# Attention and a squared-ReLU network: queries and keys of batches 3 to 7 loaded as rows in SBUF and transposed there, scores in 448 columns

## The chip, the core and the metric

The kernel runs on one core of one Trainium2 chip. The time is device microseconds of one execution; three runs of the kernel before gave a median of 371.77 us, the lowest 371.64 and the highest 372.14. All inputs and the output lie in DRAM as float32; the matrices are worked on as float16 with sums in float32.

## The reference

`q`, `k` and `v` are `[8, 12, 448, 64]`: 8 batches, 12 heads, 448 positions, 64 columns a head. Attention has one added term in its denominator, and its output goes through two matrix products with a squared ReLU between them:

```python
def _attn_ref(q, k, v):
    scale = 1.0 / np.sqrt(q.shape[-1])
    scores = scale * np.matmul(q, k.transpose(0, 1, 3, 2))
    m = np.max(scores, axis=-1, keepdims=True)
    e = np.exp(scores - m)
    attn = e / (np.sum(e, axis=-1, keepdims=True) + np.exp(-m) + 1e-09)
    return np.matmul(attn, v)

def _moe_ref(x, w_in, w_out):
    h = x @ w_in            # [3584, 768] @ [768, 2048]
    r = np.maximum(h, 0.0)
    return (r * r) @ w_out  # [3584, 2048] @ [2048, 768]

x = attn_out.transpose(0, 2, 1, 3).reshape(8 * 448, 12 * 64)
```

The output is `[3584, 768]`. Dividing numerator and denominator by `exp(-m)` shows that no maximum is needed: the kernel computes `exp(scores)` and divides by one plus its sum.

## The kernel before

**How the work is cut.** A batch has three *quads* of four heads. A quad's 448 keys are seven *chunks* of 64. For one chunk, `quad_scores` multiplies the chunk's keys with all queries of the quad's four heads; these are products with 64 rows and 64 columns of TensorE's array each, so four of them lie side by side in its four 64x64 quadrants, and the result is one PSUM tile `sp` of two banks. `quad_exp` (ScalarE) takes the exponential of the tile into a buffer `et`. `add_quad` (VectorE, four steps, L442 to L448) adds the chunks' exponentials up into a tile `half`, `sums_of_quad` lets TensorE sum over the keys (a product with a matrix of ones), `quad_z` and `quad_reciprocal` (ScalarE) make the reciprocal by a logarithm and an exponential. `values_step` multiplies one chunk's exponentials with its values, and `quad_x` (VectorE, L488) scales the sum into `xt`, the transposed input of the network. Matrix products of the network are the pieces `J` (first product, through L666, with sums and differences of blocks so that seven block products do the work of eight) and `o` (`out_piece`, second product). `out_first` and `out_second` move a finished tile of 128 tokens by 384 columns from PSUM to a buffer `ot` (five of them), and `store` writes it to DRAM.

**The order is written out by hand.** Three lists of steps, each a letter with numbers, are run one after another: the first (batches 0 to 2 come in, the network's first product of batches 0 and 1), the second (rest of batches 1 to 3), and `CYCLE`, run once with the scores of batches 4 and 5 and once with those of 6 and 7. A step puts its instructions at the end of its engines' queues, so the order of steps is the order on every engine; engines wait for one another only through the tiles. The letters that matter here are `s` (scores of a chunk), `e` (its exponential), `a`, `S`, `Z`, `M`, `v`, `X` as above in order, `o`, `O`, `Q` (a tile of output and its store) and `d` (a load). In the lists `d` counts through `LOADS`; in the cycle it is `following`, which turns a number into a load for one of the next batches. At the end stand the remaining products of batches 6 and 7 and the last tile, stored in pieces of 384, 256 and 128 columns.

**How queries and keys come in.** TensorE needs them with the 64 columns of a head on the partitions, so they have to be transposed. For batches 0 to 2 (`ON_PE`) they are loaded in natural order and transposed on TensorE; there the row of the token 7p + t is kept as column p of the block t, and a chunk is one such block. For batches 3 to 7 three steps stand in place of that. `stage(b)` (L145 to L160, issued on POOL) copies the batch's q and k from DRAM to DRAM as float16. `transposed_load(b, i)` (L167, issued on SP) reads a copy in rows of 128 values and writes it transposed into `qk`: one plane of q, one of k, and a second plane of k moved by one position, because a row of 128 values holds two neighbouring tokens of the head, and keys and queries lie in halves by odd and even token. `tail_keys(b)` (L189, POOL) copies the keys of the last chunk together, four copies a batch. The queries' two halves are why a score product there has 224 columns, and a chunk eight products:

```python
which, x = (1, h * n + c // 2) if c % 2 == o else (2, h * n + c // 2 + c % 2)
keys = qk[r, which, x:x + 190:3]
mm(sp[64 * i:64 * i + 64, o, j * n:(j + 1) * n], keys, qk[r, 0, h * n:(h + 1) * n], start=True, stop=True)
```

For the batches 0 to 2 it is four products of 448 columns. `load_v_quads` (L98 to L112) brings the values in the order that the chunks have: one transfer for batches 0 to 2, four for the others. `store` (L543 to L552) undoes the order of the tokens: a tile of 128 columns of the transposed token order is 128 rows of the output at a stride, of 7 rows for batches 0 to 2, of 2 for the others. With stride 7 a run has 64 rows, so a tile is two transfers; with stride 2 a run has 224 rows, and a tile is one transfer or, across a border, two.

**Buffers and queues.** `qk` has two buffers, `v` two, `flat` two (first quads, and the copied tail keys `kms`). The POOL queue issues all loads, in the order of the steps; the SP queue issues the transposes and the stores. In each queue a transfer waits for the one eight before it. Free parts of `qk` are used again: `small_sums` puts sums of the first product into the third plane of batch 2's, `slot` gives nine places for kept partial sums in the last part, and `wout_sum` the sums of the second weight matrix.

Of the kernel before, what the change touches and what calls it, by code (L numbers as in the profile page):

```python
# [10 lines left out]
FP32 = mybir.dt.float32  # L11
FP16 = mybir.dt.float16
# [5 lines left out]
def kernel(  # L18
# [20 lines left out]
    COLS = H * S // 2 + 16  # L39
# [14 lines left out]
    flat = ctx.enter_context(tc.tile_pool(name="flat", bufs=2))  # L54
# [26 lines left out]
    vns, qks, xts, naturals, stages = {}, {}, {}, {}, {}  # L81
# [16 lines left out]
    def load_v_quads(b, g0=0, g1=NQ):  # L98
        if b not in vns:
            vns[b] = v_pool.tile([128, 2, NQ, KC, D], FP16, name="vn")  # L100
        vn = vns[b]
        if b in ON_PE:
            if g1 - g0 == NQ:
                nc.gpsimd.dma_start(out=vn.rearrange("p j g c d -> p (j g) (c d)"), in_=by_pairs["v"][b])
            else:
                nc.gpsimd.dma_start(out=vn[:, :, g0].rearrange("p j c d -> p j (c d)"), in_=by_pairs["v"][b, :, g0::NQ])  # L106
            return
        for i in range(2):
            rows_ = vn[64 * i:64 * i + 64].rearrange("p j g c d -> p (j g) (c d)")
            for c0, c1 in ((0, KC - 1), (KC - 1, KC)):  # L110
                src = v[:, :, 64 * c0:64 * c1].rearrange("b (hp i) (p t) d -> b i p hp (t d)", i=2, t=c1 - c0)
                nc.gpsimd.dma_start(out=rows_[:, :, c0 * D:c1 * D], in_=src[b, i])  # L112
# [14 lines left out]

    def load_first_second():
        for name in "qk":
            f = naturals[name, 0, 0, 1] = flat.tile([128, KC, D], FP16, name=f"flat{name}")  # L130
            nc.gpsimd.dma_start(out=f.rearrange("p c d -> p (c d)"), in_=by_pairs[name][0, :, NQ])  # L131
# [10 lines left out]
    HSD = H * S * D  # L142
    FRONT, TOTAL = D, HSD + 16 * 2 * D

    def stage(b):  # L145
        for n, t in (("q", q), ("k", k)):
            st = nc.dram_tensor(f"stage_{n}{b}", (TOTAL,), FP16, kind="Internal").ap()
            stages[n, b] = st
            src = t.rearrange("b h s d -> (b h s d)")
            lo = b * HSD - FRONT  # L150
            hi = min(lo + TOTAL, B * HSD)
            m = (hi - lo) // 1024 * 1024
            for x, y in ((lo, lo + m), (lo + m, hi)):
                if y > x:
                    w = min(y - x, 1024)
# [942 lines left out]
```

## Time and profile before

| | us |
|---|---|
| median of three runs (lowest, highest) | 371.77 (371.64, 372.14) |
| span of the profiled execution | 372.7 |
| TensorE matmul (PE) busy | 362.5 |
| TensorE weight load (PEld) busy | 249.0 |
| ScalarE (ACT) busy | 281.8 |
| VectorE (DVE) busy | 276.6 |
| GpSimd (POOL) busy | 62.2 |

The profile holds one execution; its span is 0.9 above the median of the runs. The POOL queue's transfers were 24752 packets with 22.62 MB and 38.8% of the time of the 16 DMA engines, the SP queue's 49952 packets with 21.59 MB and 27.3%.

How its lines are read: a group of instructions stands as line, engine, operation, output and inputs, tile shapes, "x" and the count, then after a bar the summed busy time in us, the mean of one in ns, and the idle time just before them with what ended it. A line of a timeline has the start and the length in us, then the same names. A line of transfers has their count, the KB of each and the median us from issue to landing. The chain of waits follows the work that ended last back from the last instruction, each step to what released it; "issue" is time in which an engine waited for nothing that the profile shows. L94 is the helper `mm`, through which most matmuls are issued, so its groups are told apart by their tiles: `sp` scores and row sums, `mp` all else. PEclk, the granted clock, is a share of full speed.

### The profile page before, as it was taken

Reading aid. Unit: us, or ns where it says so; the run is one execution under the profiler, and the core shown is the slowest. Engines: PE = TensorE matmul, PEld = TensorE weight load, DVE = VectorE, ACT = ScalarE, POOL = GpSimd, SP = SyncE. Lnnn points to the kernel's source line nnn. Section 1 sums busy time; section 2 is a strip of 40 time slices with the busy share of each in tenths; the row PEclk is TensorE's granted clock in tenths of the full one; section 3 lists DMA queues with packets and bytes.
Section 4 is the critical chain, followed back from the end, with each engine's and each line's share of the span. In section 5 each row is a group of like instructions: output and inputs, shape, how many; then the busy total and the mean of one; then the engine's idle time right before and its main releaser. Section 6 shows DMA issues by size and latency. Waiting matters only on the chain.

```text
span 372.7 us, 13667 instructions
## 1 busy us (share of the span) xinstructions
PE 362.5 (97%) x6024; PEld 249.0 (67%) x6024; DVE 276.6 (74%) x485; ACT 281.8 (76%) x412; POOL 62.2 (17%) x96
## 2 busy tenths in 40 slices
PE   8679999999999999999999999999999999999996
PEld 4557566669977665557799975557777765555564
DVE  2688897998987774876888783777888776886441
ACT  5799888986899664689999746579999748784221
POOL 8443170400300150400201061300200000000000
PEclk9999999999999999999999999999999999999999
DMA  8999999999884999924327879864122210001232
GB/s 137 202 206 205 204 148 204 223 226 207 150 171 85 203 162 203 147 28 94 71 54 157 133 129 197 154 72 98 47 67 50 63 46 20 2 0 44 84 84 87
DMA packets 75051, 45.31 MB, mean 122 GB/s; under 512 B 47472, under 2 KB 72944, under 8 KB 74992
## 3 DMA queue, kind: packets, MB, share of 16 engines
q0 software_dynamic: 24752, 22.62, 38.8%
q1 hardware_dynamic: 49952, 21.59, 27.3%
q8 instruction: 47, 0.77, 0.9%
q10 hardware_dynamic: 288, 0.23, 0.2%
q14 instruction: 12, 0.10, 0.1%
HBM read 45.69 MB, written 17.93 MB: 171 GB/s over the span
## 4 chain that ended last, share of the span: by engine, by line
PE 89%; ACT 5%; DMA 3%; POOL 1%; issue 1%; DVE 1%; POOLq 0%; DVEq 0%
PE mp L94 42%; PE mp L666 37%; PE sp L94 9%; ACT et L258 3%; DMA nn<-in_k_dram 3%; PE mp L208 1%; ACT rcp L369 1%; ACT rcp L376 1%; POOL nn L118 1%; DVE half L446 0%; DVE half L448 0%; ACT ot L577 0%; POOL vn L106 0%; ACT rcp L372 0%; POOL flatk L131 0%
## 5 line engine op out<-in xcount | busy, mean ns | idle before, releaser
L258 ACT ACTIVATE et<-sp 128x896 f16<-128x896 f32 (+2 forms) x173 | 145.3, 900 | 8.6 <-PE sp L94 7.9
L94 PE MATMUL mp<-wout,gs 64*64 64x384 f16 (+1 forms) x2736 | 138.9, 322 | 0.3 <-issue 0.3
L94 PEld LDWEIGHTS <-gs 64*64 64x64 f16 (+1 forms) x2736 | 87.5, 107 | 21.9 <-issue 1.1
L666 PEld LDWEIGHTS <-win 128*128 128x128 f16 x480 | 46.4, 98 | 33.6 <-issue 1.2
L94 PE MATMUL sp<-qk 64*64 64x224 f16 (+1 forms) x1056 | 55.9, 273 | 1.8 <-ACT et L258 1.1
L666 PE MATMUL mp<-xt,win 128*128 128x448 f16 (+1 forms) x288 | 54.2, 329 | 0.0
L94 PEld LDWEIGHTS <-qk 64*64 64x64 f16 x1056 | 34.2, 114 | 14.0 <-issue 5.7
L189 POOL COPY flatq<-qk 64x384 f16<-64x384 f16 x20 | 15.1, 753 | 159.3 <-DMA qk<-stage_k 158.8
L94 PE MATMUL mp<-et,vn 64*64 64x448 f16 (+1 forms) x616 | 38.8, 345 | 0.0
L666 PE MATMUL mp<-et,win 128*128 128x448 f16 x144 | 32.8, 352 | 0.0
L579 DVE TENSOR_SCALAR ot<-mp 128x384 f32<-128x384 f32 x34 | 18.9, 556 | 18.3 <-PE mp L94 17.3
L666 PE MATMUL mp<-et,nn 128*128 128x448 f16 (+1 forms) x160 | 32.3, 350 | 0.0
L666 PEld LDWEIGHTS <-nn 128*128 128x128 f16 x216 | 21.0, 98 | 14.7
L669 ACT ACTIVATE qk<-mp 128x448 f32<-128x448 f32 (+1 forms) x33 | 16.7, 531 | 16.0 <-PE mp L666 15.9
L583 DVE SCALAR_TENSOR_TENSOR ot<-mp,ot 128x384 f32<-128x384 f32 x42 | 23.4, 557 | 6.6 <-ACT ot L577 3.9
L488 DVE TENSOR_TENSOR xt<-mp,rcp 128x448 f16<-128x448 f32 x42 | 24.2, 617 | 4.6 <-ACT rcp L467 2.7
L94 PEld LDWEIGHTS <-vn 64*64 64x64 f16 x756 | 22.7, 107 | 6.8 <-issue 1.3
L718 ACT ACTIVATE gs<-mp 128x448 f16<-128x448 f32 x28 | 14.2, 542 | 15.0 <-PE mp L666 13.3
L663 DVE CUSTOM_DVE_ANT_0 gs<-mp,rcp 128x448 f16<-128x448 f32 x24 | 14.2, 619 | 13.0 <-ACT rcp L669 7.4
L442 DVE TENSOR_TENSOR half<-et 128x1792 f16<-128x1792 f16 x21 | 23.0, 1095 | 0.9 <-ACT et L258 0.9
L713 ACT ACTIVATE gs<-gs 128x448 f16<-128x448 f16 (+1 forms) x36 | 22.4, 657 | 1.1 <-DVE gs L663 1.1
L444 DVE TENSOR_TENSOR half<-half,et 128x1792 f16<-128x1792 f16 x21 | 22.9, 1090 | 0.4
(102 smaller groups left out, 452.5 us busy)
## 6 DMA issues: line engine op xcount, KB each, us to landing
out_dram<-ot SPq DMA_DIRECT2D x52, 96.0 KB, 3.3
out_dram<-ot SPq DMA_DIRECT2D x19, 192.0 KB, 2.0
win<-in_moe_w_in_dram POOLq DMA_DIRECT2D x8, 384.0 KB, 11.9
wout<-in_moe_w_out_dram POOLq DMA_DIRECT2D x4, 768.0 KB, 12.2
vn<-in_v_dram POOLq DMA_DIRECT2D x10, 288.0 KB, 5.6
stage_q<-in_q_dram POOLq DMA_DIRECT2D x4, 676.0 KB, 11.8
stage_k<-in_k_dram POOLq DMA_DIRECT2D x4, 676.0 KB, 14.9
nn<-in_q_dram POOLq DMA_DIRECT2D x8, 224.0 KB, 9.0
```

Of the source, the lines that this page charges most:

```text
L94: return nc.tensor.matmul(out_, lhsT, rhs, start=start, stop=stop)
L189: nc.gpsimd.tensor_copy(km[rows_].rearrange("p h (x o) -> p h x o", o=2)[:, :, :, odd], src[:, :, S // 2 - 32:S // 2])
L258: nc.scalar.activation(out=out_, in_=in_, func=AF.Exp, scale=scale)
L442: nc.vector.tensor_add(esq[m], a[:, 0:w], a[:, w:2 * w])
L444: nc.vector.tensor_add(esq[m], esq[m], z[:, 0:w])
L488: nc.vector.tensor_mul(xts[b][:, 2 * g + i, :], xqs[m][i][:, 0:S], zqs[m][:, i, :])
L579: nc.vector.tensor_scalar(out=ot, in0=op[:, 0:w], scalar1=OUT_SCALE, scalar2=None, op0=ALU.mult)
L583: nc.vector.scalar_tensor_tensor(out=ot, in0=lo[:, 0:w], scalar=OUT_SCALE, in1=ot, op0=ALU.mult, op1=ALU.add)
L663: nc.vector._custom_dve(TENSOR_ADD_SAT, out=out_, in0=ps, in1=t, s0=3.0e38, s1=0.0)
L666: nc.tensor.matmul(out_, lhsT=lhsT, rhs=rhs, start=begins and first, stop=last, skip_group_check=not begins)
L669: nc.scalar.activation(out=t[:, 0:w], in_=src[:, 0:w], func=AF.Copy, scale=scale_)
L713: nc.scalar.activation(out=out_, in_=out_, func=AF.Square)
```

## The change

The kernel after holds all batches in the token order of batches 0 to 2, and no DRAM copies are made.

- `load_rows(b, n, j)` takes the place of `stage`. A new tile `rows` (one buffer) has q in its partitions 0 to 63 and k in 64 to 127; partition p holds, for a head pair c and a block t, the token 7p + t of head c and beside it that of head c + 6, 128 values. Each of the 24 transfers a batch loads one head of one tensor, in pieces of 64 values (128 bytes as float16), and casts on the way. `load_all_rows(b)` issues all of them on POOL.
- `transposed_load(b, n)` has two transfers a batch, q and k, from `rows` to `qk`, SBUF to SBUF; the second key plane and `tail_keys` go, and `qk` has two planes.
- `quad_scores` has one form, four products of 448 columns, and `of_column` one order. `load_v_quads` loads a batch in one transfer, and `store` has stride 7 for all tokens.
- The loads are called at other places in the lists: those of batch 3 to 5 in the second list are renumbered (rows of batch 3 stay where its staging was; the values of batch 3 stand where they stood, and batch 4's rows, which followed them directly, now come after batch 3's transposes), and `following` has a batch's two transposes, values and the rows of the batch after next in another order and at other places.
- Buffers: `flat` has four, all of one size, and `small_sums` uses them; `slot` has its places in two `qk` buffers and the `rows` buffer, and `wout_sum` the rest of these.

```diff
...
-    COLS = H * S // 2 + 16
+    COLS = H * S // 2
...
-    flat = ctx.enter_context(tc.tile_pool(name="flat", bufs=2))
+    flat = ctx.enter_context(tc.tile_pool(name="flat", bufs=4))
+    rows_pool = ctx.enter_context(tc.tile_pool(name="rows", bufs=1))
...
-    vns, qks, xts, naturals, stages = {}, {}, {}, {}, {}
+    vns, qks, xts, naturals, rows_of = {}, {}, {}, {}, {}
...
-        if b in ON_PE:
-            if g1 - g0 == NQ:
-                nc.gpsimd.dma_start(out=vn.rearrange("p j g c d -> p (j g) (c d)"), in_=by_pairs["v"][b])
-            else:
-                nc.gpsimd.dma_start(out=vn[:, :, g0].rearrange("p j c d -> p j (c d)"), in_=by_pairs["v"][b, :, g0::NQ])
-            return
-        for i in range(2):
-            rows_ = vn[64 * i:64 * i + 64].rearrange("p j g c d -> p (j g) (c d)")
-            for c0, c1 in ((0, KC - 1), (KC - 1, KC)):
-                src = v[:, :, 64 * c0:64 * c1].rearrange("b (hp i) (p t) d -> b i p hp (t d)", i=2, t=c1 - c0)
-                nc.gpsimd.dma_start(out=rows_[:, :, c0 * D:c1 * D], in_=src[b, i])
+        if g1 - g0 == NQ:
+            nc.gpsimd.dma_start(out=vn.rearrange("p j g c d -> p (j g) (c d)"), in_=by_pairs["v"][b])
+        else:
+            nc.gpsimd.dma_start(out=vn[:, :, g0].rearrange("p j c d -> p j (c d)"), in_=by_pairs["v"][b, :, g0::NQ])
...
+    def flat_tile():
+        return flat.tile([128, DCH // 2 * FIRST], FP16, name="flat")
     def load_first_second():
...
-            f = naturals[name, 0, 0, 1] = flat.tile([128, KC, D], FP16, name=f"flat{name}")
-            nc.gpsimd.dma_start(out=f.rearrange("p c d -> p (c d)"), in_=by_pairs[name][0, :, NQ])
+            f = flat_tile()[:, 0:S]
+            naturals[name, 0, 0, 1] = f.rearrange("p (c d) -> p c d", d=D)
+            nc.gpsimd.dma_start(out=f, in_=by_pairs[name][0, :, NQ])
...
-    HSD = H * S * D
-    FRONT, TOTAL = D, HSD + 16 * 2 * D
-    def stage(b):
...
-    PLANES = (("q", FRONT, H * S // 2), ("k", FRONT, H * S // 2), ("k", 0, COLS))
-    def transposed_load(b, i):
-        qk = qk_of(b)
-        n, x, c = PLANES[i]
+    def load_rows(b, n, j):
+        if b not in rows_of:
+            rows_of[b] = rows_pool.tile([128, DCH * KC * 2 * D], FP16, name="rows")
+        dst = rows_of[b][64 * n:64 * n + 64].rearrange("p (c t j d) -> p c t j d", c=DCH, t=KC, j=2)
+        for c in range(DCH):
+            nc.gpsimd.dma_start(out=dst[:, c, :, j], in_=(q, k)[n][b, DCH * j + c].rearrange("(p t) d -> p t d", t=KC))
+    def load_all_rows(b):
+        for n in range(2):
+            for j in range(2):
+                load_rows(b, n, j)
+    def transposed_load(b, n):
...
-            out=qk[:, i, 0:c],
-            in_=stages[n, b][x:x + c * 2 * D].rearrange("(r c) -> r c", c=2 * D),
+            out=qk_of(b)[:, n].rearrange("p (r x) -> p r x", x=64),
+            in_=rows_of[b][64 * n:64 * n + 64],
...
     def transposed_loads(b):
-        for i in range(3):
-            transposed_load(b, i)
-    kms = {}
-    def tail_keys(b, planes=(1, 2)):
...
     def qk_of(b):
...
-            qks[b] = qk_pool.tile([128, 3, COLS], FP16, name="qk")
+            qks[b] = qk_pool.tile([128, 2, COLS], FP16, name="qk")
...
     def first_cast(raw, name, c0, c1, act):
...
-            naturals[name, 0, 0, 0] = flat.tile([128, KC, D], FP16, name=f"flat{name}")
+            naturals[name, 0, 0, 0] = flat_tile()[:, 0:S].rearrange("p (c d) -> p c d", d=D)
...
-    def of_column(e, m, j):
-        if QUADS[m][0] in ON_PE:
-            return e.rearrange("p (j x) -> p j x", j=2)[:, j]
-        return e.rearrange("p (o j x) -> p j o x", o=2, j=2)[:, j]
+    def of_column(e, j):
+        return e.rearrange("p (j x) -> p j x", j=2)[:, j]
...
     def quad_scores(m, c):
...
-        if b in ON_PE:
-            for i in range(2):
-                for j in range(2):
-                    r = slice(64 * j, 64 * j + 64)
-                    x = (2 * g + i) * S
-                    mm(sp[64 * i:64 * i + 64, j, 0:S], qk[r, 1, x + 64 * c:x + 64 * c + 64],
-                       qk[r, 0, x:x + S], start=True, stop=True)
-        else:
-            n = S // 2
+        for i in range(2):
...
-                for i in range(2):
-                    for o in range(2):
-                        r = slice(64 * o, 64 * o + 64)
-                        h = 2 * NQ * j + 2 * g + i
-                        if c == KC - 1:
-                            keys = kms[b][r, h, :]
-                        else:
-                            which, x = (1, h * n + c // 2) if c % 2 == o else (2, h * n + c // 2 + c % 2)
-                            keys = qk[r, which, x:x + 190:3]
-                        mm(sp[64 * i:64 * i + 64, o, j * n:(j + 1) * n], keys,
-                           qk[r, 0, h * n:(h + 1) * n], start=True, stop=True)
+                r = slice(64 * j, 64 * j + 64)
+                x = (2 * g + i) * S
+                mm(sp[64 * i:64 * i + 64, j, 0:S], qk[r, 1, x + 64 * c:x + 64 * c + 64],
+                   qk[r, 0, x:x + S], start=True, stop=True)
...
-                mm(zp[64 * j:64 * j + 64, i, 0:S], ones[r], of_column(es[r], m, j), start=True, stop=True)
+                mm(zp[64 * j:64 * j + 64, i, 0:S], ones[r], of_column(es[r], j), start=True, stop=True)
...
-                mm(xqs[m][i][64 * j:64 * j + 64, 0:S], vns[b][r, j, g, c, :], of_column(e[r], m, j),
+                mm(xqs[m][i][64 * j:64 * j + 64, 0:S], vns[b][r, j, g, c, :], of_column(e[r], j),
...
-            step = KC if b in ON_PE else 2
-            rows = out[b * S:(b + 1) * S, n0:n1].rearrange("(p t) m -> t p m", t=step)
-            t, p = c % S // (S // step), c % S % (S // step)
-            m = min(S // step - p, end - c)
+            rows = out[b * S:(b + 1) * S, n0:n1].rearrange("(p t) m -> t p m", t=KC)
+            t, p = c % S // 64, c % 64
+            m = min(64 - p, end - c)
...
-             + [lambda: stage(3), lambda: transposed_loads(3), lambda: tail_keys(3), lambda: load_v_quads(3),
-                lambda: stage(4), lambda: transposed_loads(4), lambda: tail_keys(4), lambda: load_v_quads(4), lambda: stage(5)])
+             + [lambda: load_all_rows(3), lambda: transposed_loads(3), lambda: load_v_quads(3),
+                lambda: load_all_rows(4), lambda: transposed_loads(4), lambda: load_v_quads(4), lambda: load_all_rows(5)])
...
     def small_sums(xsum, y):
-        xsum[y] = qks[2][:, 2, (y - 1) * HC * FIRST:y * HC * FIRST].rearrange("p (c n) -> p c n", c=HC)
+        xsum[y] = flat_tile().rearrange("p (c n) -> p c n", c=HC)
...
+    osum = {}
...
     def slot():
...
-            scratch.append(qk_pool.tile([128, 3 * COLS // 2], FP32, name="qk"))
-        n = slots[0] = (slots[0] + 1) % 9
-        return scratch[0][:, n * S:n * S + S]
+            t, u = (qk_pool.tile([128, COLS], FP32, name="qk") for _ in range(2))
+            w = rows_pool.tile([128, COLS], FP32, name="rows")
+            osum["u"], osum["w"] = u, w
+            scratch.extend(t[:, n * S:n * S + S] for n in range(COLS // S))
+            scratch.extend(u[:, COLS - n * S:COLS - n * S + S] for n in (2, 1))
+            scratch.append(w[:, COLS - S:COLS])
+        slots[0] += 1
+        return scratch[slots[0] % len(scratch)]
...
-        o4,12,14 s58 o4,14,16 v3,0 S3 v3,1 e58 O4,0 v3,2 v3,3 Z3 Q4 v3,4 a4,1 s59 v3,5 d26 d27 o3,0,2 s60 v3,6 a4,2 M3 o3,2,4 o3,4,6 e59
+        o4,12,14 s58 o4,14,16 v3,0 S3 v3,1 e58 O4,0 v3,2 v3,3 Z3 Q4 v3,4 a4,1 s59 v3,5 d25 o3,0,2 s60 v3,6 a4,2 M3 o3,2,4 o3,4,6 e59
...
-        o5,10,12 o5,12,14 e63 a5,0 s64 o5,14,16 S4 O5,1 J0,1 A0 Q5 d24 d25 e64 y4 J1,1 J0,2 w1 J0,6 J1,2 C0 A1 J1,6 J0,5 U0 U1 B0 C1 w6 a5,1
+        o5,10,12 o5,12,14 e63 a5,0 s64 o5,14,16 S4 O5,1 J0,1 A0 Q5 d24 d26 e64 y4 J1,1 J0,2 w1 J0,6 J1,2 C0 A1 J1,6 J0,5 U0 U1 B0 C1 w6 a5,1
...
         def following(n):
-            ahead, what = ((1, n) if n < 6 else (2, 6) if n < 7 else (1, 6) if n < 8 else (2, n - 8))
+            what, ahead = {0: (0, 1), 1: (1, 1), 2: (2, 1), 3: (3, 2), 4: (0, 2), 5: (1, 2), 6: (2, 2), 7: (3, 3)}[n]
...
-            if t < B and (n != 7 or b > FIRST_PERIOD):
-                if what < 3:
+            if t < B:
+                if what < 2:
...
-                elif what < 5:
-                    tail_keys(t, (what - 2,))
-                elif what == 5:
+                elif what == 2:
...
-                    stage(t)
+                    load_all_rows(t)
...
-        d7 d2 J0,1 y3 J1,1 y4 A0 J0,2 C0 A1 d6 J1,2 C1 J0,6 J1,6 U0 J0,5 U1 J1,5 J0,7 B0 J0,3 D0 J1,7 B1 J0,4 G1 J1,3 D1 E0 J1,4 F1 E1 d0 J2,1
+        d0 d1 J0,1 y3 J1,1 y4 A0 J0,2 C0 A1 d3 J1,2 C1 J0,6 J1,6 U0 J0,5 U1 J1,5 J0,7 B0 J0,3 D0 J1,7 B1 J0,4 G1 J1,3 D1 E0 J1,4 F1 E1 J2,1
...
-    osum, gsum = {}, {}
+    gsum = {}
...
     def wout_block(r, n):
...
-            if which == 3:
-                osum["t"] = qk_pool.tile([128, 3, COLS], FP16, name="qk").rearrange("p n x -> p (n x)")
-            t = e_pool.tile([128, RUN * 2 * S], FP16, name="et") if which < 3 else osum["t"][:, (which - 3) * HF * HALF:]
-            osum[which] = t[:, 0:HF * HALF].rearrange("p (f n) -> p f n", f=HF)
+            if which < 3:
+                t = e_pool.tile([128, RUN * 2 * S], FP16, name="et")[:, 0:HF * HALF]
+            else:
+                t = osum["uw"[which - 3]][:, 0:HF * HALF // 2].bitcast(FP16)
+            osum[which] = t.rearrange("p (f n) -> p f n", f=HF)
...
```

More of the change, by code (lines that the diff above doesn't have):

```diff
@@ L173, in transposed_loads @@
     def transposed_loads(b):
[L174 to L190 removed]
+        for n in range(2):
+            transposed_load(b, n)
     def qk_of(b):
         if b not in qks:
[L196 removed]
+            qks[b] = qk_pool.tile([128, 2, COLS], FP16, name="qk")
         return qks[b]
```

49 lines of the change are left out of this document (12 added, 37 removed).

## The prediction

> **What bounds the kernel now.** I read the page's busy shares first, then the chain of work that ended last, then busy time by stretch, then the chain again in detail. The busy shares and the chain's shares by engine:
>
> ```profile
> PE 362.5 (97%) x6024; PEld 249.0 (67%) x6024; DVE 276.6 (74%) x485; ACT 281.8 (76%) x412; POOL 62.2 (17%) x96
> PE 89%; ACT 5%; DMA 3%; POOL 1%; issue 1%; DVE 1%; POOLq 0%; DVEq 0%
> ```
>
> TensorE (PE) is busy 97% of the span and is 89% of the chain. The mean could hide a stage with another limit, so I took stretches from the one where batch 3 starts. The columns are stretch, length, PE busy, granted clock, DMA share, GB/s:
>
> ```profile
> 100.00:134.00 34.00, 33.56 (x849) 1.00 0.76 138
> 165.60:219.90 54.30, 54.30 (x1428) 1.00 0.50 102
> 251.40:305.40 54.00, 54.00 (x1427) 1.00 0.23 64
> ```
>
> The two late stretches are the score parts of the two cycles (batches 4 and 5, then 6 and 7): PE is never idle there. In the first, with batch 3, it idles 34.00 - 33.56 = 0.44 us. So whatever else the change frees is worth nothing in the late stretches unless PE's own columns get cheaper, and it can cost whatever makes PE wait. About 0.2% (0.74 us) is what a measurement of this kernel can tell from no change.
>
> **Score matmuls.** Five batches of three quads of seven chunks make 105 chunks; each goes from eight matmuls of 224 columns to four of 448. Four of them (64x64 quadrants) run side by side, so a chunk is 448 columns of PE time before and after. Batches 1 and 2 use the wide form already. In the chain's detail, "sp" pieces there are wide, and those of batch 7 narrow (some matmul records are missing, so counts are low):
>
> ```profile
> 71.19 0.65 PE mp L94 x16
> 71.84 0.19 PE sp L94 x4
> 74.55 1.30 PE mp L94 x32
> 281.22 0.65 PE mp L94 x12
> 281.88 0.19 PE sp L94 x6
> 286.27 0.70 PE mp L94 x12
> ```
>
> Both forms take 0.19. A finer reading: from 71.19 to 74.55 lie four equal periods of output piece plus chunk, 0.840 each; from 281.22 to 286.27 lie six, 0.842 each. The difference, 0.002 with about 0.003 of rounding, times 105 is 0.2 us. I take -0.2, between -0.5 and 0.
>
> The Trainium skill, page "TensorEngine Tiling (Array Packing)", section "Instruction Overhead", says each matmul has an overhead of about 60 cycles. By that, 420 fewer matmuls would be worth far more than these rows show; that is a rival below.
>
> The 420 weight loads that go with them lie behind the matmuls:
>
> ```profile
> L94 PEld LDWEIGHTS <-qk 64*64 64x64 f16 x1056 | 34.2, 114 | 14.0 <-issue 5.7
> ```
>
> At 34.2/1056 = 0.032 each they would be 13.6 us if nothing covered them; the equal 0.19 above says that everything does. I cost them at nothing.
>
> **What POOL stops doing.** The 20 key copies go. They touch the path at one place, just ahead of the second cycle's start:
>
> ```profile
> 128.06 1.52 POOL L189 COPY flatq<-qk 64x384 f16<-64x384 f16 x2 [25.12 <-DMA qk<-stage_k]
> 128.18 0.92 DVE L446 TENSOR_TENSOR half<-half 128x896 f16<-128x896 f16 x1
> 129.21 0.80 DVE L448 TENSOR_TENSOR half<-half,et 128x896 f16<-128x896 f16 x1
> 129.57 0.36 PE L94 MATMUL mp<-et,vn 64*64 64x448 f16 x4
> 130.06 0.38 PE L94 MATMUL sp<-half,ones 64*64 64x448 f16 x4
> L446 DVE TENSOR_TENSOR half<-half 128x896 f16<-128x896 f16 x21 | 13.6, 646 | 0.3
> ```
>
> Beside the copies two DVE adds took 0.92 and 0.80 where the mean is 0.65, and PE's row sums, which need them, started 0.49 after the matmuls before, 0.30 more than the 0.19 these stream. Without the copies I take -0.3 (-0.3 to 0). The staging copies go too. While they ran, PE waited once for nothing that the profile shows:
>
> ```profile
> 102.40 0.55 POOL L156 DMA_DIRECT2D stage_k<-in_k_dram  x1
> stage_k<-in_k_dram POOLq DMA_DIRECT2D x1, 676.0 KB, 9.5
> 110.58 0.49 PE mp L94 x12
> 111.07 0.31 issue
> 111.38 0.36 PE mp L94 x4
> ```
>
> The staging lands at 102.40 + 9.5 = 111.9, and PE starts again at 111.38. If the traffic caused it, 0.3 goes; but the new loads put traffic into the same stretch for longer. I take -0.1, between -0.3 and +1 (such a wait in three places).
>
> **Stores.** All batches now store rows in the order of batches 0 to 2, so each 128-row tile leaves as two stores of 64 rows, where most tiles of batches 3 to 7 left as one. SP's issues of a pair, and of a single:
>
> ```profile
> 107.51 1.11 SPq L551 DMA_DIRECT2D out_dram<-ot  x2
> 256.61 0.33 SPq L551 DMA_DIRECT2D out_dram<-ot  x1
> 369.51 1.09 SPq L551 DMA_DIRECT2D out_dram<-ot  x2
> 369.94 0.28 ACT L577 ACTIVATE ot<-mp 128x128 f32<-128x128 f32 x1 [0.46 <-PE mp L94]
> out_dram<-ot SPq DMA_DIRECT2D x1, 64.0 KB, 1.5
> ```
>
> A pair holds SP 1.11, a single 0.33. In the middle nothing waits for this: output tiles come 2 us and more apart, and five buffers stand behind them. At the very end it is bare. The last two tiles' stores start at 369.51 and about 370.25 now, and the last lands 1.5 later. With pairs the first holds SP until 369.51 + 1.11 = 370.62, the last issue starts some 0.5 into the second pair, 371.15, and lands 1.5 later: 0.9 after today's. Bounds: 0.35, were each issue 0.33, and 1.1, a whole second pair. I take +0.9; no cover is there.
>
> **Loads.** Per batch, two or so staging transfers per tensor and three transposes become 24 row loads of 56 KB (pieces of 128 bytes) and two transposes; v goes from four transfers to one. Prices: POOL's issue of a v load of 384 pieces, and a stretch of a v load with mostly 128-byte pieces:
>
> ```profile
> L112 POOL DMA_DIRECT2D vn<-in_v_dram x20 | 13.0, 668 | 17.1 <-PE mp L94 16.9 <-issue 0.3
> DMA packets 569, 0.17 MB, mean 140 GB/s; under 512 B 414, under 2 KB 569, under 8 KB 569
> ```
>
> 24 issues of 0.67 are 16.1 us. The second row is a stretch of 1.2 us (157.0 to 158.2): 2.1 ns a packet, so 448 pieces take 0.94 and 24 loads 22.6. A batch's rows take 16 to 23 us; I take 20, about the middle, as either side can limit. The transposes from SBUF are in no row. Nearest is one from DRAM of the same volume, 6.0 from issue to landing; I take 6, with half and double of it, 3 and 12, as bounds.
>
> The rows have one buffer, so from batch 3 on everything is a chain: rows, transposes, next rows. Batch 3 is the tight one:
>
> ```profile
> 51.45 0.88 POOL L104 DMA_DIRECT2D vn<-in_v_dram  x1
> vn<-in_v_dram POOLq DMA_DIRECT2D x1, 672.0 KB, 18.4
> 86.80 4.78 SPq L167 DMA_TRANSPOSE qk<-stage_q  x1
> qk<-stage_k SPq DMA_TRANSPOSE x10, 6.0
> 100.43 1.52 POOL L189 COPY flatq<-qk 64x384 f16<-64x384 f16 x2 [1.31 <-DMA qk<-stage_k]
> 101.16 0.36 PE L94 MATMUL sp<-qk 64*64 64x224 f16 x8
> 200.83 0.40 PE L94 MATMUL mp<-et,vn 64*64 64x448 f16 x4
> ```
>
> Batch 2's v lands at 51.45 + 18.4 = 69.9, and the rows queue behind it. They have landed at 69.9 + 20, a tenth more for the stores beside them, and 2 of latency: 94. SP reaches q's transpose at 86.8, so only k's is left: 94 + 6 = 100. PE wants both at 101.16, and before, too, the last plane had landed only at 100.43. So batch 3 just holds, at no cost, by 1 us. Behind the waiting transposes on SP stand stores that are not due before 107.51. Batch 4's rows, moved behind these transposes, have landed at 100 + 22 = 122 and are transposed at 128; batch 5's at 150 and 156; batch 6's rows at 178, and batch 5's v, queued behind them on POOL, some 6 later at 184. PE first uses that v at 200.83: 16 us to spare. SP is free again at 156, before the next stores at 170. Cost: nothing, unless a batch takes 5 us more.
>
> **Moves with no price.** The small sums go into the flat pool, the kept partial sums and the last output sums into two query-key buffers and the row buffer: same instructions, same shapes, and the row buffer is last read by batch 7's transposes, by the same chain about 250, with its first reuse after 305.40.
>
> **The sum.** -0.2 - 0.3 - 0.1 + 0.9 = +0.3 us on the profiled 372.7. The profiled span is 0.9 above the 371.77 median of the runs, so the runs come to 372.1.
>
> **Rivals.** First, slower: batch 3's keys are late. The mechanism is the single row buffer's first round behind batch 2's v; it decides from 101.16 on. With rows at 23 and the transpose at 8, k lands at 69.9 + 25 + 2 + 8 = 105, and PE stands for 4 us: 376. For it: 1 us of slack and an unmeasured transpose. Against: q's half is done early, and rows at 16 land everything by 96. It spans 373 to 378.
>
> Second, slower: the small loads do not overlap. The trace has stores landing 1.5 after issue at best; 24 in a row are 36 us, k's keys come at 69.9 + 36 + 2 + 6 = 114, 13 late: 385. Against it stand four v loads:
>
> ```profile
> 153.62 2.61 POOL L112 DMA_DIRECT2D vn<-in_v_dram  x4
> vn<-in_v_dram POOLq DMA_DIRECT2D x2, 288.0 KB, 4.9
> vn<-in_v_dram POOLq DMA_DIRECT2D x2, 48.0 KB, 4.6
> ```
>
> Issued within 2.61, each landed 4.6 to 4.9 after its issue, so they ran side by side. The Trainium skill, page "DMA: Bandwidth & Descriptors", section "Rules for kernel authors", speaks for it: transfers under 64 KB pay mostly overhead and should be joined. The trace agrees only where nothing overlaps.
>
> Third, faster: every matmul has a fixed price that 420 fewer do not pay. If it were that of 60 columns, 0.19 x 60/448 = 0.025 each, 10.7 us would go: 361. Against: the equal 0.19 above. It is the result of the page's rule on instruction overhead.
>
> Fourth, slightly faster: all three waits go (-0.5 - 0.3 - 0.3) and the last stores cost only 0.35: -0.75, 371.0. That the change does not do what it says can be left to the transposes: it does, or the scores would have no keys.
>
> **How the numbers follow.** Forecast 0.55 (371.3 to 373.0 by its own bounds), late keys 0.30, small loads 0.03, page's overhead 0.02, slightly faster 0.10. Range: 371.0, the fourth case, to 375.5, three quarters of the late keys. Faster by over 0.2% (under 371.03): 0.02 + 0.08 = 0.10. Slower (over 372.51): 0.33 of the late cases and a quarter of the forecast, 0.14: 0.47. The same: 0.43.
>
> **What would show it.** In the profile after: score pieces at 0.19 in the chain; batch 3's first scores within 0.5 us of 101; the row loads of a batch landing within 20 to 25 us; transposes landing 6 us after issue; the PE row sums near 130 without the 0.3; and two pairs of stores after the last PE matmul, the last issued near 371. Wrong it would be if PE waits for a transpose anywhere, if the end after the last matmul has not grown, or if the late stretches change by more than 0.3.

## The result and the profile after

The kernel after took 372.97 us (median of 8 runs, 372.12 to 373.90), the kernel before beside it 371.80 (8 runs, 371.43 to 372.87). The ratio is 1.0031, with a 95% interval of 1.0016 to 1.0046: 1.15 us slower, between 0.6 and 1.7. Measured once more on another chip, in a later experiment, it was 1.0009 (0.9991 to 1.0027). So the change costs something between nothing and 0.46%; the two ratios lie at 0.31% and 0.09%.

Busy times and the chain by engine, of the kernel after:

```profile
PE 361.8 (97%) x5604; PEld 237.6 (64%) x5604; DVE 274.7 (74%) x485; ACT 281.7 (76%) x412; POOL 116.5 (31%) x167
PE 90%; ACT 4%; DMA 2%; POOL 2%; issue 1%; POOLq 0%
```

PE bounds it as before. Two things have to be known for the comparison. First, a run's time here is the span plus 1.8 us (the profiled run of after: span 371.9, time 373.71), so before's profiled execution with its span of 372.7 was not 0.9 above the median but about 2.7. Its delay is in the first 33 us: the first score exponential of batch 1 started at 33.1 there, at 30.7 after, and at 30.3 in a later profile of before with other stores. Second, the two traces therefore have to be compared from a common point. The chain of waits gives one: its pieces of the network's first product are 168 matmuls each and have the same length everywhere. Before:

```profile
84.62 16.21 PE mp L666 x168
134.18 31.89 PE mp L666 x168
219.93 31.89 PE mp L666 x168
305.48 31.89 PE mp L666 x168
```

After:

```profile
81.98 16.21 PE mp L619 x168
130.65 31.89 PE mp L619 x168
217.11 31.89 PE mp L619 x168
302.54 31.89 PE mp L619 x168
```

From start to start, and from the last start to the span's end (372.7 and 371.9):

| stretch | before | after | difference |
|---|---|---|---|
| batch 3 | 49.56 | 48.67 | -0.89 |
| first cycle (batches 4, 5) | 85.75 | 86.46 | +0.71 |
| second cycle (batches 6, 7) | 85.55 | 85.43 | -0.12 |
| end | 67.22 | 69.36 | +2.14 |

In batch 3 two of before's waits are gone, and no new one came: products due at about 110.9 began 0.49 late at 111.38, and row sums due at about 129.8 began 0.30 late at 130.06. (They are not the same in every execution: in the later profile of before, batch 3 takes 49.19.) In the first cycle there is one new wait, for nothing that the profile shows:

```profile
187.98 0.36 PE L95 MATMUL mp<-et,vn 64*64 64x448 f16 x4
188.17 0.36 PE L95 MATMUL sp<-qk 64*64 64x448 f16 x4
188.36 0.82 PE L95 MATMUL mp<-wout,gs 64*64 64x384 f16 x15
189.89 0.32 PE L95 MATMUL mp<-wout,gs 64*64 64x384 f16 x1 [0.71 <-issue]
```

Sixteen such products follow one another in 0.65 elsewhere; here the last begins at 189.89, some 0.9 late. The second cycle, with its 42 score chunks, is 0.12 shorter. And the end is 2.14 longer though PE's work there is the same. The timeline of the stores on SP, and then of the last two evictions on ACT, after:

```profile
362.41 1.75 SPq L504 DMA_DIRECT2D out_dram<-ot  x3
364.20 2.94 SPq L504 DMA_DIRECT2D out_dram<-ot  x3
367.24 1.19 SPq L504 DMA_DIRECT2D out_dram<-ot  x2
368.53 1.18 SPq L504 DMA_DIRECT2D out_dram<-ot  x2
```

```profile
366.16 0.38 ACT L530 ACTIVATE ot<-mp 128x256 f32<-128x256 f32 x1 [1.30 <-PE mp L95]
367.01 0.28 ACT L530 ACTIVATE ot<-mp 128x128 f32<-128x128 f32 x1 [0.46 <-PE mp L95]
```

SP issues ten stores from 362.41 to 369.71 without a pause. One of the three that follow 364.20 takes much longer than the others, which take 0.5 to 0.6:

```profile
364.90 1.60 SPq L504 DMA_DIRECT2D out_dram<-ot  x1
```

The tile evicted at 366.54 starts to leave at 367.24, the one evicted at 367.29 only at 368.53. Before, the last store started 0.03 after its eviction. From the last eviction to the end it is 4.6 now, 2.5 before.

The row loads on the page of after:

```profile
L146 POOL DMA_DIRECT2D rows<-in_q_dram x60 | 42.8, 721 | 94.7 <-DMA qk<-rows 82.1
...
rows<-in_q_dram POOLq DMA_DIRECT2D x60, 56.0 KB, 3.5
```

The transfers issued from 84 to 100, with the two transposes that batch 3 needs, and from 180.5 to 187.2, with batch 5's values:

```profile
qk<-rows SPq DMA_TRANSPOSE x2, 8.1
```

```profile
vn<-in_v_dram POOLq DMA_DIRECT2D x1, 672.0 KB, 9.9
```

POOL issues the 24 loads of a batch back to back, 0.72 each, 17 us a batch, and the median load lands 3.5 after its issue: they overlap. The last loads of a batch can land later. Those of batch 4 were issued from 98.71 to 115.06, and the last landed at 123.16, 8.1 after its issue, while the next transpose, issued at 114.35, was under way. From the first issue to the last landing the rows of batches 4 to 7 took 20.4 to 24.5. The transposes of batch 3 were issued at 84.42 and 90.48 and landed 8.6 and 7.7 later, so the keys at 98.1. PE's first product with them starts at 98.51, without a wait. All ten transposes landed 7.0 to 11.9 after their issue, 8.5 in the median.

### The profile page after: what moved, and what is told of

Read it like the earlier page. It is cut to its first block, busy times and chain, and to the rows that moved or that the text cites. A ratio compares the mean times of both kernels' runs of the same rounds, so it can differ in the third digit from the quotient of the medians.

```text
span 371.9 us, 12973 instructions
## 1 busy us (share of the span) xinstructions
PE 361.8 (97%) x5604; PEld 237.6 (64%) x5604; DVE 274.7 (74%) x485; ACT 281.7 (76%) x412; POOL 116.5 (31%) x167
## 4 chain that ended last, share of the span: by engine, by line
PE 90%; ACT 4%; DMA 2%; POOL 2%; issue 1%; POOLq 0%
PE mp L95 43%; PE mp L619 37%; PE sp L95 9%; ACT et L230 3%; DMA nn<-in_k_dram 2%; PE mp L180 1%; POOL nn L112 1%; ACT rcp L348 1%; ACT rcp L341 0%; POOL flat L129 0%; POOL vn L106 0%; ACT rcp L344 0%; ACT gs L459 0%; POOL ident masks.py:199 0%; ACT ot L530 0%
## 5 line engine op out<-in xcount | busy, mean ns | idle before, releaser
L146 POOL DMA_DIRECT2D rows<-in_q_dram x60 | 42.8, 721 | 94.7 <-DMA qk<-rows 82.1
L95 PE MATMUL sp<-qk 64*64 64x448 f16 (+1 forms) x756 | 62.1, 332 | 1.9 <-ACT et L230 0.7
L146 POOL DMA_DIRECT2D rows<-in_k_dram x60 | 42.6, 719 | 0.0
L95 PEld LDWEIGHTS <-qk 64*64 64x64 f16 x756 | 24.0, 106 | 14.4 <-issue 6.9
L532 DVE TENSOR_SCALAR ot<-mp 128x384 f32<-128x384 f32 x34 | 18.9, 555 | 17.8 <-PE mp L95 17.6
L95 PEld LDWEIGHTS <-vn 64*64 64x64 f16 x756 | 23.6, 107 | 9.3 <-issue 0.8
L622 ACT ACTIVATE qk<-mp 128x448 f32<-128x448 f32 (+1 forms) x30 | 15.2, 532 | 13.3 <-PE mp L619 13.2
```

The costliest lines, as they stand in the source:

```text
L95: return nc.tensor.matmul(out_, lhsT, rhs, start=start, stop=stop)
L146: nc.gpsimd.dma_start(out=dst[:, c, :, j], in_=(q, k)[n][b, DCH * j + c].rearrange("(p t) d -> p t d", t=KC))
L532: nc.vector.tensor_scalar(out=ot, in0=op[:, 0:w], scalar1=OUT_SCALE, scalar2=None, op0=ALU.mult)
L622: nc.scalar.activation(out=t[:, 0:w], in_=src[:, 0:w], func=AF.Copy, scale=scale_)
```

## The experiments

"Above" and "below" are medians beside runs of the kernel before on the same chip. Theory A: SP's issue of the store pairs makes the end longer. Theory C: the wait at 189 is TensorE's instruction fetch, held up by load traffic. Theory E: batch 3's keys come so tight that some executions wait for them.

**One transfer for both runs of a tile** (`e1_joined`).

```diff
-            t, p = c % S // 64, c % 64
-            m = min(64 - p, end - c)
+            t = c % S // 64
+            m = min(KC - t, (end - c) // 64)
...
-            nc.sync.dma_start(out=rows[t, p:p + m, :], in_=ot[o:o + m, :])
-            c += m
+            nc.sync.dma_start(out=rows[t:t + m], in_=ot[o:o + 64 * m, :])
+            c += 64 * m
```

> The kernel after, with each 128-row output tile stored by one transfer where its two runs of 64 rows lie in one batch (24 of 28 tile positions). Theory A (the loss is SP's issuing of the last store pairs): in the trace after, SP issues without a pause from 362.41 to 369.71 and the last matmul piece ends its eviction at 367.29, 4.6 before the end, against 2.5 before; with one issue of 0.35 to 0.6 a tile, the end falls back to 2.5 after the last eviction, and the time is about 1.5 to 2.1 less than after's 1.15 over before: 0.4 to 1.0 below before. Theory B (the loss lies ahead of the tail, in the wait at 188.85 and the late keys): the tail was paid for by pieces of DMA work that stay the same, so the gain is under 0.5 and the time stays 0.6 or more above before.

Measured: 445.86, ratio 1.197 (1.193 to 1.201). Neither theory had this. The window after the last eviction, its columns being stretch, length, busy times, granted clock, DMA share and GB/s, and SP's last five stores:

```profile
428.00:442.00 14.00, 0.00 (x0) 0.00 (x0) 0.00 (x0) 0.00 (x0) 0.00 (x0) 0.50 0.13 47
```

```profile
417.89 16.50 SPq L504 DMA_DIRECT2D out_dram<-ot  x5
```

With nothing but these stores under way, 0.13 of 16 DMA engines is two of them, and an issue holds SP for 3.3 us on the average. Most of the loss lies before the end, in two waits of PE: 17.8 for batch 3's keys, whose rows landed at 111.1 where after had 82.6, and 27.7 for values. The Trainium skill, page "DMA: Bandwidth & Descriptors", section "Why a DMA increments its semaphore by 16 and not by 1", says that a transfer runs on the largest number of engines up to 16 that divides the slowest dimension's size on both sides; in the output that dimension is two here. The share of 0.13 agrees. The run says nothing on A, since it put a worse limit in the place of the one to be removed.

**The second half of the last seven tiles through ACT** (`e2_two_queues`).

```diff
-            nc.sync.dma_start(out=rows[t, p:p + m, :], in_=ot[o:o + m, :])
+            queue = nc.scalar if end > B * S - 128 * 7 and o else nc.sync
+            queue.dma_start(out=rows[t, p:p + m, :], in_=ot[o:o + m, :])
```

> The kernel after, with the second 64-row store of each of the last seven tiles issued by ACT instead of SP. Theory A (issuing on SP bounds the tail): the two halves are issued side by side, the last of them about 0.6 after the last eviction, so 1 to 2 us less than after. Theory B (not the issue but the landing of many small transfers, or something ahead of the tail): within 0.4 of after, 0.7 or more above before.

Measured: 371.89, before 371.98; ratio 0.9997 (0.9983 to 1.0011). That is 1.1 less than after's 372.97, which was measured apart. In the timeline of its profile (span 371.1) the last pair leaves at once:

```profile
367.80 0.28 ACT L531 ACTIVATE ot<-mp 128x128 f32<-128x128 f32 x1 [0.63 <-PE mp L95]
368.11 0.47 SPq L505 DMA_DIRECT2D out_dram<-ot  x1
368.11 0.50 ACTq L505 DMA_DIRECT2D out_dram<-ot  x1
```

From 368.08, the last eviction's end, to 371.1 it is 3.0, where after had 4.6. The stores move the same bytes in the same pieces, and the last one lands 2.0 after its issue where it was 1.9 in after. So it was the issue and not the landing: theory A. Before, with 2.5, the last store landed 1.5 after its issue; that part of the difference stays.

**The kernel before with pairs at the end** (`e3_before_pairs`).

```diff
-            step = KC if b in ON_PE else 2
+            step = KC if b in ON_PE or end > B * S - 128 * 7 else 2
```

> The kernel before, with its last seven tiles stored in runs of 64 rows at a stride of 7, two transfers each, as after; those tiles' rows stand in another order in the output. Theory A: +1.5 to +2.2 over before, with SP issuing without a pause in the last 7 us. The prediction's term would make it +0.9 (0.35 to 1.1). Theory B: within 0.4 of before.

Measured: 373.91, 1.93 above before; ratio 1.0062 (1.0037 to 1.0087). That is theory A's size, about twice the prediction's term. But SP does not issue without a pause here. It is done with the pair before these two at 366.26 and stands until 366.74, and no issue takes longer than 0.6. The last eviction runs from 367.17 to 367.45:

```profile
366.74 1.11 SPq L551 DMA_DIRECT2D out_dram<-ot  x2
367.94 1.19 SPq L551 DMA_DIRECT2D out_dram<-ot  x2
```

So only the last pair waits, 0.5, for the one before it, and the last store starts 1.1 after the last eviction. That is the delay that the prediction had. The store lands 1.9 after its issue instead of 1.5, and from there to the end it is 1.4 where before and after have 0.9; nothing here shows why.

**Scores in 224 columns** (`e4_narrow`).

```diff
-                mm(sp[64 * i:64 * i + 64, j, 0:S], qk[r, 1, x + 64 * c:x + 64 * c + 64],
-                   qk[r, 0, x:x + S], start=True, stop=True)
+                for y in ((0, S // 2) if b >= 3 else (0,)):
+                    w = S // 2 if b >= 3 else S
+                    mm(sp[64 * i:64 * i + 64, j, y:y + w], qk[r, 1, x + 64 * c:x + 64 * c + 64],
+                       qk[r, 0, x + y:x + y + w], start=True, stop=True)
```

> The kernel after, with the scores of batches 3 to 7 in eight products of 224 columns again, four more weight loads and products a chunk, 420 in all. The prediction's theory (only columns count): 0.2 to 0.5 above after, so 1.3 to 1.7 above before, with equal periods of output piece and chunk of 0.842. Rival (a fixed price of about 60 columns a product): 10.7 above after.

Measured: 374.44, 1.5 above after's 372.97; ratio to before 1.0079 (1.0048 to 1.0110), so 2.5 above before where 1.3 to 1.7 was expected. The rival with a fixed price (10.7) falls. The second cycle, which has no waits, shows the products' own cost:

```profile
221.81 31.89 PE mp L621 x168
307.38 31.88 PE mp L621 x168
```

85.57 against 85.43 for 42 chunks: 0.14, so 0.35 for all 105. The rest stays open: there are 840 more instructions, products and weight loads, and the profile shows two waits. But the profiled run was the slowest of the seven (377.78), so the median run need not have them. One was for the keys, one for nothing shown, and after that one the granted clock fell to 0.57 (the column before the last two):

```profile
100.00 0.40 PE L95 MATMUL sp<-qk 64*64 64x224 f16 x8 [0.43 <-DMA qk<-rows]
126.31 3.18 PE L95 MATMUL mp<-wout,gs 64*64 64x384 f16 x48 [1.94 <-issue]
```

```profile
127.00:131.00 4.00, 4.00 (x64) 2.52 (x60) 1.72 (x3) 1.30 (x2) 0.00 (x0) 0.57 0.80 137
131.00:135.00 4.00, 3.99 (x96) 2.51 (x92) 1.95 (x4) 2.35 (x3) 1.25 (x2) 1.00 0.43 99
```

**Batch 5's values ahead of batch 6's rows** (`e5_v_first`).

```diff
-        d0 d1 J0,1 y3 J1,1 y4 A0 J0,2 C0 A1 d3 J1,2
+        d0 d1 J0,1 y3 J1,1 y4 A0 J0,2 C0 A1 d2 d3 J1,2
...
-        A6 C6 C7 J7,6 d2 J6,6
+        A6 C6 C7 J7,6 J6,6
```

> The kernel after, with the step that loads batch 5's values put ahead of the one that loads batch 6's rows (a cycle later the same for batch 7's values). In after, that values load is issued at 181.03 behind 24 row loads and lands 9.9 later; the instruction fetch of TensorE in that stretch starts at 187.3, 376 instructions after the one before where 250 are usual, and PE waits 0.88 at 188.85 for nothing that the profile shows. Theory C (the fetch queues behind load traffic): the load goes out at about 152 to 156, where PE runs large products and fetches seldom; the wait at 188.85 is gone or under 0.2, and the time is 0.4 to 0.9 below after. Theory D (the wait comes from PE's own queue or from a store): it stays where it is, and the time is that of after within 0.3.

Measured: 372.90, before 372.06; ratio 1.0013 (0.9999 to 1.0027). Its profile has no wait of PE after 95 us, that at 189 included, as theory C has it. That the median falls by the wait's length is not shown: 0.84 above before is what after had, within the spread.

**Batch 3's transposes earlier on SP** (`e6_early`).

```diff
-        e61 e62 a4,3 s63 o5,6,8 O3,0 y3 Q3 o5,8,10
+        e61 e62 a4,3 s63 o5,6,8 O3,0 d24 y3 Q3 o5,8,10
...
-        S4 O5,1 J0,1 A0 Q5 d24 d26 e64
+        S4 O5,1 J0,1 A0 Q5 d26 e64
```

> The kernel after, with batch 3's two transposes issued on SP ahead of the stores of two output tiles instead of behind them, so from about 78 instead of 84.42. In after the keys land at 98.2, about 0.3 before PE's first product with them, and in the narrow variant PE waited 0.6 for them. Theory E (late keys are a cost in a part of the executions): keys land at 91 or earlier, batch 4's rows start then, and the median falls by 0.2 to 0.6 with less spread. Theory F (they are just in time in nearly all): within 0.2 of after. If the two waiting transposes hold up the stores too long, it is slower than after by what the output tiles then wait.

Measured: 372.68, 0.6 above before; ratio 1.0021 (1.0005 to 1.0037). The transposes start at 76.69 and 87.31, batch 4's rows at 94.73 instead of 98.71, and the two delayed tiles cost PE nothing. Against after's 372.97 the gain is within the spread: inconclusive in time.

**All three edits** (`e7_three`).

> The kernel after with three edits: the second half of each of the last seven tiles stored through ACT, batch 5's and 7's values loaded ahead of the rows, batch 3's transposes ahead of two tiles' stores. If the three are independent (theories A, C, E): 1.1 + 0.4 to 0.9 + 0 to 0.6 below after, so 0.4 to 1.4 below before. If the waits only move (a fetch late at another place, as from 80.88 and 110.73 before to 188.85 after): 1.1 below after, equal to before within 0.3.

Measured: 371.30, before 372.06; ratio 0.9983 (0.9971 to 0.9995). It is 0.8 faster than before, and beside after in the later runs 1.5 faster than that. Its profile has no wait of PE after 95.

**POOL copies put back** (`e8_pool_copies`, issued right behind batch 4's rows).

```diff
+    def pool_copies(n):
+        for _ in range(n):
+            t = spare[0:64].rearrange("p (h x o) -> p h x o", h=12, o=2)
+            keys = qks[3][0:64, 1].rearrange("p (h x) -> p h x", h=12)
+            nc.gpsimd.tensor_copy(t[:, :, :, 0], keys[:, :, 192:206])
```

> The kernel after, with 44 copies of 64x168 on POOL added behind batch 4's rows, from about 116 on, of keys that nothing reads; the result is unchanged. The prediction's theory (POOL copies slow the adds of VectorE that run beside them): the adds of 128x896 at about 125 take 0.75 to 0.95 instead of 0.61 to 0.62, and PE's row sums after them start late by up to 0.3. Rival (the slow adds in the profile before had another cause): the adds stay at 0.61 to 0.62 beside the copies.

A single run took 373.97. The 44 copies ran from 114.41 to 138.1 (39 of them stand in the view), and the adds beside them took what they take in after without copies, 0.61 to 0.62:

```profile
114.41 21.59 POOL L587 COPY spare<-qk 64x168 f16<-64x168 f16 x39
```

```profile
124.74 0.62 DVE L400 TENSOR_TENSOR half<-half 128x896 f16<-128x896 f16 x1
125.46 0.63 DVE L402 TENSOR_TENSOR half<-half,et 128x896 f16<-128x896 f16 x1
```

The rival holds for these copies; those of before were of another shape (64x384) and reached the adds at another moment. What the copies did delay was batch 5's rows, which stand behind them on POOL, and through the chain of rows and transposes batch 5's values: PE waited for them until 198.34, by the view of the waits (total, times, longest):

```profile
PE mp L95 <- DMA vn<-in_v_dram: 1.3, 1, 1.3
```

**After and two variants side by side** (`e9_after_again`, unchanged; `e10_inner`, the two order edits without the divided stores; `e11_three_again`).

> The kernel after, unchanged, beside the next two on one chip. All theories: 1.0016 to 1.0046 times before, as in its first measurement; its profile shows whether the wait near 188.85 and the keys' landing near 98 return (theory C: a wait of 0.5 to 1.2 near 189 in this profile as well; theory D has no place for it).

> The kernel after with batch 5's and 7's values ahead of the rows and batch 3's transposes ahead of two tiles' stores; all stores through SP as in after. Theories C and E together: 0.5 to 1.1 below after, so between before and 0.6 above it, and no wait of TensorE between 95 and 300. If the waits only move: within 0.3 of after.

> The kernel with the three edits again, beside after and the variant without the divided stores. Theory A: 1 to 1.5 below the variant without them, 0.4 to 1.2 below before, with 3.1 from the last eviction to the end instead of 4.4.

Measured beside 372.28 for before: 372.88 (1.0009, 0.9991 to 1.0027), 372.74 (1.0010, 0.9993 to 1.0026), 371.38 (0.9978, 0.9962 to 0.9993). In after's new profile the wait is there again: a product begins at 189.91, after 0.78 of idle time. The chain of `e10_inner`:

```profile
82.61 16.21 PE mp L619 x168
131.28 31.89 PE mp L619 x168
216.72 31.89 PE mp L619 x168
302.15 31.89 PE mp L619 x168
```

The first cycle takes 85.44, the length of the second, where after's two profiles have 86.46 and 86.53. Of the profiles with the values behind the rows, three have the wait near 189 (0.7 to 1.0 of idle time: after twice, and the variant with two queues). The others, in which loads or products stand some us earlier or later (the early transposes, the copies on either half of the partitions, the narrow scores, the joined stores), have none there, and none of the four with the values first has one. This points to the values' transfer meeting a fetch; that the two must meet is argued, not shown. In the medians, though, the order edits are worth 0.14, within the spread and short of the 0.5 to 1.1 expected, and the divided stores 1.36.

**The copies on the other partitions** (`e12_pool_upper`).

> The kernel after with the 44 POOL copies on partitions 64 to 127 instead of 0 to 63. Adds of 128x896 beside copies were slow (0.80) where the copy then running was the one on the upper half in the variant of before with store pairs, and at 0.61 beside the one on the lower half. If the half decides: adds at 0.75 or more here. If not: 0.61 to 0.63, and what made them slow stays open.

A single run took 372.11; the adds of 128x896 beside the copies took 0.62 and 0.63. For these copies the half does not decide.

## Why the prediction was right, and where it was not

The time lay within the range, and the sum had the right sign: the stores at the end outweigh what the middle gains. It is 0.9 above the forecast of 372.1, and just inside the 371.3 to 373.0 given for it. (Those two are not what the terms' bounds add up to: from -0.75 to +2.1, so 371.0 to 373.9.) That it came so near is in part luck, since the stores cost more than their upper bound and waits of similar size went and came. One of the prediction's own signs of being wrong did show: the first cycle, one of the stretches that were to stay within 0.3, grew by 0.7. Step by step:

- **Score matmuls, -0.2.** Right. The second cycle gives 0.12 for 42 chunks, the narrow variant 0.14, so 0.30 to 0.35 for 105, inside the stated 0 to 0.5. The rival with a fixed price a matmul is refuted.
- **POOL copies, -0.3.** The wait is gone in after, but the reason given is not shown. In the kernel before with pairs the copies ran at the same place, one add took 0.80 and the other 0.61, and the row sums started without a wait; copies of another shape put back left the adds at 0.62. What made before's adds take 0.92 and 0.80 stays open.
- **Staging wait, -0.1 (-0.3 to +1).** The wait before 111.38 went, and one of 0.9 came at 189, behind the values' transfer. What was expected of the new traffic as an outer bound, one such wait, is what after's two profiles show, in a stretch that the prediction held to be free of waits.
- **Stores, +0.9.** The step that was mis-sized. The mechanism was the one named, SP's issue of a pair, and the delay that it reckoned is there: in the profiles without a long issue (before with pairs, the narrow scores, `e10_inner`) the last store starts 1.1 after the last eviction, where it was 0.03. Two things were not in the sum. The last store lands 1.9 after its issue instead of 1.5. And in most profiles of after and its variants that store through SP, an issue some 2.4 before the last eviction takes 1.0 to 1.9 instead of 0.6; then the pair behind it starts late too. In after it takes 1.60: the pair due at 366.54 starts 0.7 late, the last 1.2 late, its second store at 369.11, and with the landing that makes the +2.1 of the profile. From the last eviction to the end it is 3.9 to 4.9 in the eight profiles with this tail, where before had 2.5, so 1.4 to 2.4 more. The run of before with pairs gave +1.9, the one that divides the stores gave 1.4 back. What makes the one issue long is not shown.
- **Loads.** POOL's issue took 17 us a batch, and rows had landed 20.4 to 24.5 after the first issue: the 20 to 25 that were predicted. The transposes took 8.5 where 6 was taken. For batch 3 two errors cancel, which was luck: its rows were issued from 49.85 on beside batch 2's values and had landed at 82.55 (85.2 when the two profiles are laid together at batch 3's start), where 94 was taken; but "only k's is left" fell, since SP reached q's transpose at 84.42 and both came one after the other, 13.7 in all. So batch 3 held, by 0.4 us instead of 1, and in the narrow variant it did not. Of the 16 us to spare for batch 5's values (issued at 181.03, landed at 190.96, first used at 197.95) there were 7.
- **The base.** The span's 0.9 above the median was taken as an offset; it was an execution that began late, while a run is 1.8 more than its own span. The forecast for the runs was made by difference, so it did not suffer.

For the runs, +1.4 to +2.4 for the stores and -0.3 for the scores leave between +0.1 and -0.9 to the waits, if the whole is to be +1.2. What the waits are worth in the median run is the open part: after's first cycles give the order edits 1.0 and 1.1, the medians 0.14. In both of after's measurements the profiled run was longer than the median (373.71 against 372.97, 373.98 against 372.88), so the wait at 189 may be rarer than the profiles suggest. That was not settled.

## What to carry to other kernels

At the end of a kernel count every issue of the storing queue back to the point where it last stood idle, not just the last ones; a second queue for half of them paid at once. A transfer that is one large piece can go ahead of a train of small ones if it only has to wait for a free buffer; here that took the wait out of the profiles, but the medians do not show a gain. Look at what else uses the DMA engines then: TensorE's instructions come that way too. A layout that removes work in the middle but cuts the last stores in two is judged at its end.

## What the runs showed of the hardware

- **A late instruction fetch is the likely cause of TensorE's wait at 189.** The queue `q8 instruction` moved 44 packets of 16 KB in after, one for every 255 of TensorE's 11208 matmuls and weight loads. None was served between 180.5 and 187.2, while the loads filled the DMA engines; then one was, and PE stood at 189:

```profile
q0 software_dynamic: 2034, 0.71, 102.9%
q1 hardware_dynamic: 184, 0.23, 11.0%
```

```profile
q0 software_dynamic: 152, 0.13, 56.9%
q1 hardware_dynamic: 102, 0.12, 29.3%
q8 instruction: 1, 0.02, 4.3%
```

  The first fence has the queues from 180.5 to 187.2 (packets, MB, share of 16 engines' time), the second those from 187.2 to 188.6. Counted in the traces, this fetch started 377 instructions after the one before; in the two other profiles with the wait it was 433 and 425, in the profiles without it at most 337 in the same place. The count alone does not decide: elsewhere one of 400 passed without a wait (`e8_pool_copies`, at 214.9). The Trainium skill, page "Runtime: NRT & Kernel Launch", section "Instruction fetch mechanics", has the 16 KB and 256 instructions, and holds the fetch to be mostly hidden; these profiles speak against that.
- **A pause costs twice.** After the pause of 1.94 us that ended at 126.31 in the narrow variant, PE ran at half clock from 127.3 to 130.7 (0.57 on the mean of 127 to 131), which by an estimate from these two times cost another 1.7 us. The Trainium skill, page "TensorE: Matmul & The Clock Gate", section "Part 1: The HAM clock gate (the "warmup" mystery)", has an idle window of about 3.4 us before the gate closes; here the pause was shorter than that, and the half clock began 2.9 after the pause did.
- **Two stores of 64 rows hold SP for 1.1 us, one of 128 rows for 0.35**, at the same bytes. In the run with joined stores, whose leading dimension is two, the stores kept 0.13 of 16 DMA engines busy.
